# Gated mix of a state-space layer and a feed-forward layer: the first 512 rows of even x brought in by transposing DMAs

## The chip, the cores and the metric

The kernel runs on one core of a Trainium2 chip. The metric is device microseconds for one execution; the time before is the median of three runs. The profile is one execution of the same program, with times in microseconds from its span's start. PE is TensorE (PEld its weight loads), DVE is VectorE, ACT is ScalarE, POOL is GpSimd, SP is SyncE. SP and ACT each have a DMA queue; SPq and ACTq are the instructions that issue DMAs on them.

## The reference

x has 2048 rows of 448 columns, in bf16. Two branches read it and a gate mixes them:

```python
g = sigmoid((x * gate_w).sum(-1, keepdims=True))
# a: a complex diagonal state space; h runs over the 2048 rows
Lam_bar = exp(dt * Lam);  B_bar = ((Lam_bar - 1) / Lam)[:, None] * Bmat
h[t] = Lam_bar * h[t-1] + B_bar @ x[t]
a = 2 * real(C @ h) + x * Dskip
# b: feed-forward, F = 1792
b = silu(x @ w1) @ w2
return g * a + (1 - g) * b
```

## The kernel before

The rows of x are split into even and odd ones: `x2` has 1024 rows, each with an even row's 448 columns and then the odd row's. The tile XT holds x transposed (columns on the partitions): blocks 0 to 3 are the even columns 0 to 511, where block 3 holds 64 columns that count and 64 that belong to the odd half; blocks 4 to 7 are the odd ones. XR holds the 64 remaining columns on the other half of the partitions, so that two matmuls of 64 partitions can run side by side.

The instructions of each engine are written out by hand in program order. A small tracker (`Tracker`, L43) puts the waits: an operation waits for the last writer of each key that it reads, and for the readers of what it overwrites. DMAs are issued by SP or ACT, in the order in which the code names them, and each has a semaphore of its own.

PE's order is this. First come warm-up matmuls on constants (`warm`, L477). Then comes the first feed-forward matmul for the even rows 0 to 511 (chunk 0), for the first six blocks of 128 hidden columns, in six PSUM banks: `ffn1_first` (L427) runs the first three column blocks of x (j = 0, 1, 2), and `ffn1_rem` (L443) the remaining 64 columns, for two banks at a time, and starts the SiLU activation of them (L455, on ACT, into AT). After that the stream is made of pairs (`pair`, L373, with its matmuls at L365): the other hidden blocks of chunk 0, then chunk 1, then the state-space input projections of XT with BT (`bu_even`, `bu_odd`, `bu3_even`, `bu3_odd`) between them, and the second feed-forward matmul (L809, L794) and the output projection (L1047) behind. `mm_cols` (L469) puts three parameter rows (tile R: log_dt and the two halves of Lambda) on the partitions by four tiny matmuls inside `ffn1_first`. A chain of small DVE and ACT operations follows from them: PV (L528), dt, phf, ar, mag, and a table load for SiLU (L572).

In the head of the kernel before, natural x (rows on the partitions) for the first 512 even rows comes by six plain loads into XH, which is the first part of the tile XN, in pieces with the keys XA0 to XA3, XB0 and XB1, on the queues of SP and ACT in turn, with W1's first pieces between them (W1E, L259). PE turns each 128 x 128 tile of it (`turn_k`, L489, transposes at L491) into PSUM, and DVE copies the result into XT (`turned_k` L499, at L501; `turned_x` L504, at L507), and into XR (L571). Matmuls of `ffn1_first` stand between these transposes, the first of them on 256 columns of x only (h = 0, 1).

After the loads of the head, SP waits for the two W1 pieces of the remaining 64 columns (`gE`), and then issues all other transposing DMAs (`ldt`, L228, at L229): XT of even rows 512 to 1023 (XTe1, XTer1), the four of B into BT, XT of the odd rows (XTo0, XTr0, XTo1, XTr1). Between them stand the loads of natural x that are still missing (`load_xn`, L303): h = 0 brings the columns 512 to 895 of the first 512 rows of x2, after the BT transposes, and h = 1 the other 512 rows. Natural x is read by DVE for the gate (L650) and for the skip product (L658). The broadcast loads GWB and DB (`ld_b`, L297), which those two read, are issued on ACT's queue at the end of the head.

Of the kernel before, what the change touches and what calls it, by code (L numbers as in the profile page):

```python
# [8 lines left out]
AF = mybir.ActivationFunctionType  # L9

F32 = DT.float32
BF16 = DT.bfloat16
# [7 lines left out]
D = 448  # L20
# [2 lines left out]
NK = 1024  # L23
NKT = 8
NF1 = 6
NWARM = 20


class Dma:
# [121 lines left out]
def gated_mix(nc, A_x, A_Lambda_re, A_Lambda_im, A_B_re, A_B_im, A_C_re, A_C_im, A_log_dt,  # L151
              A_Dskip, B_x, B_w1, B_w2, gate_w, out):
    with ExitStack() as ctx:
        E = ctx.enter_context
        T = Tracker(nc, ctx)
# [76 lines left out]
        XE = [(["XTe000", "XTe001", "XTe010", "XTe011", "XTe02"], ["XTe03"]), (["XTe1"], ["XTer1"])]  # L232
        XO = [([f"XTo{h}"], [f"XTr{h}"]) for h in range(2)]

        def swap_xr(eng, h, odd):
# [18 lines left out]
        XA = ["XA0", "XA1", "XA2", "XA3", "XB0", "XB1"]  # L254
        FA, FB = 768, 1280
        x0 = x2[0:512, 0:512].rearrange("(k p) c -> p k c", p=128)
# [11 lines left out]
        def ld_wr(eng, c, later):  # L268
            p = slice(64 * c, 64 * c + 64)
            if later:  # L270
                return ld(eng, W1E[p, 3, 384:896].rearrange("p (n f) -> p n f", n=2),
                          B_w1[384:448, FA:].rearrange("p (n c f) -> p n c f", n=2, c=2)[:, :, c, :], f"W1Es{c}")
            return ld(eng, W1E[p, 3, 0:384], B_w1[384:448, 384 * c:384 * c + 384], f"W1Er{c}")

        for k, eng in enumerate(("sp", "act")):
            ld(eng, XH[:, k, 0:256], x0[:, k, 0:256], XA[k])
        for c, eng in enumerate(("sp", "act")):
            ld_w(eng, 0, 384 * c, 384 * c + 384, c)
        for k, eng in ((2, "sp"), (3, "act")):
            ld(eng, XH[:, k, 0:384], x0[:, k, 0:384], XA[k])  # L280
        ld_w("sp", 1)
        ld("act", XH[:, 0:2, 256:512], x0[:, 0:2, 256:512], XA[4])
        for i, (eng, v) in enumerate((("sp", A_log_dt), ("sp", A_Lambda_re), ("act", A_Lambda_im))):
            ld_row(eng, i, v)
        ld_w("act", 2)
        ld("sp", XH[:, 2:4, 384:512], x0[:, 2:4, 384:512], XA[5])
        gE = [ld_wr(eng, c, False) for c, eng in enumerate(("sp", "act"))]
        ld_w3("sp", 0, 2, FA, FB, "d")
        ld_w3("act", 2, 3, FA, FB, "d")
        for c, eng in enumerate(("sp", "act")):  # L290
            ld_wr(eng, c, True)
        T.op("act", lambda e: e.activation(JK[:, 0:1], HP[:, :], AF.Exp), reads=["HP"], writes=["JK0"])
        ld_w3("sp", 0, 1, FB, F_FF, "e")
        ld_w3("act", 1, 3, FB, F_FF, "e")
        BTK = [f"BT{i}" for i in range(4)] + ["BTz"]
# [1 line left out]
        def ld_b(dst, src, key):  # L297
            ld("act", dst[:, :], row(src).partition_broadcast(128).rearrange("p o n -> p (o n)"), key)

        ld_b(GWB, gate_w, "GW")  # L300
        ld_b(DB, A_Dskip, "DB")

        def load_xn(h):  # L303
            c0 = 0 if h else 512
            ld("sp", XN[:, 8 * h * D:8 * (h + 1) * D].rearrange("p (k c) -> p k c", k=4)[:, :, c0:],
               x2[h * 512:(h + 1) * 512, c0:].rearrange("(k p) c -> p k c", p=128), f"XN{h}")

        T.wait_all("sp", gE)
        ldt(XT[:, 0:3, 512:1024], x2[512:1024, 0:384], "XTe1")
# [116 lines left out]

        def ffn1_first():  # L427
            banks = [nxt() for _ in range(NF1)]
            for j, h in ((0, 0), (0, 1), (1, None), (2, None)):
                c = slice(0, 512) if h is None else slice(256 * h, 256 * h + 256)  # L430
                for n, fb in enumerate((0, 2, 4, 1, 3, 5)):
                    bank = banks[fb]
                    T.op("pe", lambda pe, fb=fb, bank=bank, j=j, h=h, c=c: pe.matmul(  # L433
                        ps[:, bank, c], W1E[:, j, ff(fb) * 128:(ff(fb) + 1) * 128], XT[:, j, c],
                        start=(h == 0), stop=(h == 0), skip_group_check=(h != 0)),
                        reads=[f"W1Ej{j}" if j else f"W1Ej0{fb % 2}"] + (
                            ["XTe02"] if j == 2 else [f"XTe0{j}{h}"] if h is not None else [f"XTe0{j}0", f"XTe0{j}1"]),
                        writes=[f"ps{bank}"])
                    if (j, h, n) in ((0, 0, 3), (0, 0, 5), (1, None, 2), (1, None, 5)):
                        yield  # L440
            yield banks

# [43 lines left out]
        PB = (6, 7, 6, 7)  # L486
        xp = [ps[:, b, 0:256].bitcast(BF16) for b in PB]

        def turn_k(j, k, b=None):  # L489
            b = PB[j] if b is None else b  # L490
            T.op("pe", lambda pe: pe.transpose(  # L491
                ps[:, b, 0:256].bitcast(BF16)[:, k * 128:(k + 1) * 128], XH[:, k, j * 128:(j + 1) * 128], ID[:, :]),
                reads=[XA[k if j < 2 or (j == 2 and k > 1) else 4 + k // 2], "ID"], writes=[f"ps{b}"])

        def turn_x(j, i):
            for k in (2 * i, 2 * i + 1):
                turn_k(j, k)

        def turned_k(j, k, b):  # L499
            c = slice(128 * k, 128 * k + 128)  # L500
            T.op("dve", lambda e: e.tensor_copy(XT[:, j, c], ps[:, b, 0:256].bitcast(BF16)[:, c]),  # L501
                 reads=[f"ps{b}"], writes=[f"XTe0{j}{k // 2}" + ("" if k % 2 else "a")])

        def turned_x(j, i=None, b=None):  # L504
            c, key = (slice(0, 512), f"XTe0{j}") if i is None else (slice(256 * i, 256 * i + 256), f"XTe0{j}{i}")
            b = PB[j] if b is None else b
            T.op("dve", lambda e: e.tensor_copy(XT[:, j, c], ps[:, b, 0:256].bitcast(BF16)[:, c]),  # L507
                 reads=[f"ps{b}"], writes=[key])

        for k in range(2):  # L510
            turn_k(0, k, 6 - k)
            turned_k(0, k, 6 - k)
        turn_x(1, 0)
        turned_x(1, 0)
        warm(2, 4)
        first = ffn1_first()
        next(first)
        for k in (2, 3):
            turn_k(0, k, k + 4)
            turned_k(0, k, k + 4)  # L520
        next(first)
        for k in (2, 3):
            turn_k(1, k, 6)
        turned_x(1, 1, 6)
        rd()
        next(first)
        T.op("pe", mm_cols, reads=["R0", "R1", "R2", "Rd", "ID"], writes=["pv"])
        T.op("dve", lambda e: e.tensor_copy(  # L528
            PV[:, :, :], ps[:, 7, 256:288].rearrange("p (t c) -> p t c", c=8)[:, :, 0:4]),
            reads=["pv", "ps7"], writes=["PV"])  # L530
        for i in range(2):
            turn_x(2, i)
        turned_x(2)
        next(first)
        for i in range(2):
            turn_x(3, i)

        names = {}

# [5 lines left out]
        def col(n):  # L545
            i = pc(n)
            return P[:, i, :]
# [7 lines left out]
        def pts(o, a, s1, s2, op0, op1, ra):  # L555
            T.op("dve", lambda e: e.tensor_scalar(col(o), a, s1, s2, op0, op1), reads=ra, writes=[o])
# [81 lines left out]
        def xblock(b):  # L638
            v = XN[:, 4 * b * D:4 * (b + 1) * D].rearrange("p (k c) -> p k c", k=4) if b > 1 else \
                XH[:, :, b * D:(b + 1) * D]  # L640
            return v, [*(XA if b < 2 else []), *([f"XN{b // 2}"] if b else [])]

        def block(tile):
            return tile // 4 if tile > 7 else tile % 2
# [516 lines left out]
        f = ffn1(2)  # L1161
# [100 lines left out]
```

## Time and profile before

| what | value |
|---|---|
| median of 3 runs | 136.64 us (136.61 to 136.76) |
| the profiled execution | 136.72 us |
| its span | 135.3 us |
| PE busy | 131.9 us, 97% |
| DVE busy | 114.2 us, 84% |
| ACT busy | 93.7 us, 69% |
| first warm-up matmul | 0.82 us |
| first matmul of ffn1_first | 3.80 us |
| first matmul of ffn1_rem | 9.79 us |

The chain that ended last is a list of pieces in order of time: what the last instruction waited for, followed back to the start. The windows give, for a stretch of time, the busy time of each engine with the number of its instructions, the granted share of the TensorE clock (PEclk), the mean busy share of the 16 DMA engines, which can exceed 1 where packets overlap, and what they moved in GB/s. The list of DMA issues gives the time from the issue to the landing.

### The profile page before, as it was taken

How to read it: one execution, taken by the hardware profiler on the slowest of the kernel's cores; microseconds unless marked ns; L12 is line 12 of the kernel's file. 1: busy time of each engine (PE TensorE's matmuls, PEld its weight loads, DVE VectorE, ACT ScalarE, POOL GpSimd, SP SyncE). 2: the span in 40 equal slices, each digit the busy share in tenths (PEclk: the TensorE clock that was granted, in tenths of full speed). 3: DMA queues.
4: the chain of work that ended last, by engine and by line, in shares of the span. 5: the costliest groups of instructions: out<-in, count | busy, mean ns of one | idle time of the engine just before them, and what ended most of it. 6: DMA issues, size and time to landing. Idle time of an engine off the chain costs nothing.

```text
span 135.3 us, 2630 instructions
## 1 busy us (share of the span) xinstructions
PE 131.9 (97%) x1072; PEld 65.7 (49%) x1073; DVE 114.2 (84%) x152; ACT 93.7 (69%) x146; POOL 15.1 (11%) x32
## 2 busy tenths in 40 slices
PE   7899999999999999999999999999999999999993
PEld 7554444444444554444445544445555555555552
DVE  1467898917899798999999999999999999994554
ACT  0369888899939999768999597797113437879200
POOL 7108768050000000000000000000000000000000
DMA  4999979999897220000122000000000000222123
GB/s 109 273 278 162 157 153 244 181 286 300 251 184 123 55 62 0 0 0 0 44 56 60 5 0 0 0 5 0 0 0 0 0 0 7 100 89 81 68 78 126
DMA packets 24928, 11.95 MB, mean 88 GB/s; under 512 B 16851, under 2 KB 24406, under 8 KB 24918
## 3 DMA queue, kind: packets, MB, share of 16 engines
q1 hardware_dynamic: 22996, 10.43, 32.3%
q10 hardware_dynamic: 1922, 1.37, 3.6%
q8 instruction: 8, 0.13, 0.4%
q14 instruction: 2, 0.02, 0.0%
HBM read 5.51 MB, written 1.84 MB: 54 GB/s over the span
## 4 chain that ended last, share of the span: by engine, by line
PE 94%; DMA 3%; DVE 1%; ACTq 1%; issue 0%
PE ps L365 44%; PE ps L794 16%; PE ps L809 16%; PE ps L1047 15%; DMA XN<-in_A_x_dram 3%; PE ps L433 3%; DVE TMPS L1071 1%; ACTq L226 1%; PE ps L491 1%; PE ps L447 1%; PE ps L472 0%
## 5 line engine op out<-in xcount | busy, mean ns | idle before, releaser
L365 PE MATMUL ps<-XT,W1E 64*128 64x512 bf16 x325 | 41.3, 376 | 0.0
L455 ACT ACTIVATE AT<-ps 128x1024 bf16<-128x1024 f32 x28 | 28.2, 1019 | 7.4 <-PE ps L365 7.2
L365 PEld LDWEIGHTS ps<-XT,W1E 64*128 64x128 bf16 x325 | 16.9, 94 | 19.0 <-ACT AT L455 0.3
L365 PE MATMUL ps<-XT,BT 64*128 64x512 bf16 x156 | 22.4, 376 | 0.0
L809 PE MATMUL ps<-W,AT 64*128 64x448 bf16 x224 | 21.5, 349 | 0.0
L794 PE MATMUL ps<-W,AT 128*128 128x448 bf16 x112 | 21.4, 353 | 0.0
L794 PEld LDWEIGHTS ps<-W,AT 128*128 128x128 bf16 x112 | 10.9, 98 | 10.5 <-issue 0.4
L809 PEld LDWEIGHTS ps<-W,AT 64*128 64x128 bf16 x224 | 10.9, 94 | 10.4
L838 ACT ACTIVATE BT<-ps,GT 128x448 bf16<-128x448 f32 x8 | 5.1, 634 | 13.2 <-PE ps L794 13.2
L894 DVE SCALAR_TENSOR_TENSOR HS<-VE,P,ps 128x512 bf16<-128x512 bf16 (+1 forms) x13 | 9.6, 780 | 3.9 <-PE ps L365 3.9
L365 PEld LDWEIGHTS ps<-XT,BT 64*128 64x128 bf16 x156 | 8.1, 94 | 9.3 <-DVE HS L894 0.4
L938 DVE TENSOR_TENSOR_SCAN G<-P,Q 128x1024 f32<-128x1024 f32 (+1 forms) x6 | 11.4, 1923 | 0.0
L1047 PE MATMUL ps<-CO,VE 128*128 128x448 bf16 (+2 forms) x63 | 11.1, 332 | 0.0
L1047 PE MATMUL ps<-CO,HS 128*128 128x448 bf16 x56 | 11.1, 352 | 0.0
L365 PE MATMUL ps<-XR,W1E 64*128 64x512 bf16 x25 | 9.2, 376 | 0.0
L1047 PEld LDWEIGHTS ps<-CO,VE 128*128 128x128 bf16 x63 | 6.0, 98 | 4.8
L1047 PEld LDWEIGHTS ps<-CO,HS 128*128 128x128 bf16 x56 | 5.5, 98 | 5.1
L891 DVE TENSOR_TENSOR Q<-G,COS 128x2048 bf16<-128x2048 f32 (+1 forms) x4 | 7.0, 1755 | 0.1
L891 DVE TENSOR_TENSOR Q<-G,SIN 128x2048 bf16<-128x2048 f32 (+1 forms) x4 | 7.0, 1750 | 0.0
L856 ACT ACTIVATE VE<-ps 128x1024 bf16<-128x1024 f32 x6 | 6.1, 1020 | 1.2 <-PE ps L365 1.2
L858 ACT ACTIVATE ps<-VE,P 128x1024 f32<-128x1024 bf16 x6 | 6.7, 1118 | 0.2
L894 DVE SCALAR_TENSOR_TENSOR VE<-HS,P,FP 128x512 bf16<-128x512 bf16 (+1 forms) x7 | 6.6, 976 | 0.1
(123 smaller groups left out, 179.1 us busy)
## 6 DMA issues: line engine op xcount, KB each, us to landing
W<-in_B_w_dram SPq DMA_DIRECT2D x2, 784.0 KB, 6.6
XN<-in_A_x_dram SPq DMA_DIRECT2D x1, 896.0 KB, 5.1
out_dram<-OT SPq DMA_DIRECT2D x8, 112.0 KB, 1.7
out_dram<-TMPS SPq DMA_DIRECT2D x7, 112.0 KB, 1.7
HS<-HS SPq DMA_DIRECT2D x4, 128.0 KB, 2.3
XN<-in_A_x_dram SPq DMA_DIRECT2D x1, 384.0 KB, 3.7
W1E<-in_B_w_dram SPq DMA_DIRECT2D x1, 256.0 KB, 5.5
W1E<-in_B_w_dram ACTq DMA_DIRECT2D x1, 256.0 KB, 5.0
```

The costliest lines, as they stand in the source:

```text
L365: ins = pe.matmul(ps[:, bank, :], w(p, j), xh(odd, h, j, p), start=start and j == js[0], stop=stop and j == js[-1], skip_group_check=seeded)
L433: T.op("pe", lambda pe, fb=fb, bank=bank, j=j, h=h, c=c: pe.matmul(ps[:, bank, c], W1E[:, j, ff(fb) * 128:(ff(fb) + 1) * 128], XT[:, j, c] ...
L455: T.op("act", lambda e: e.activation(a[:, fb:fb + n, :], ps[:, bank:bank + n, :], AF.Silu), reads=[f"ps{bank + i}" for i in range(n)], wri ...
L794: ins = pe.matmul(ps[:, bank, 0:D], a[:, fb, q * 128:(q + 1) * 128], W2[:, ff(fb), :], start=(first and fb == 0), stop=(fb == NFB - 1), sk ...
L809: ins = pe.matmul(ps[:, bank, 0:D], a[p, fb, q * 128:(q + 1) * 128], W2[p, ff(fb), :], start=(start and fb == 0), stop=(not start and fb = ...
L838: T.op("act", lambda e: e.activation(bs(tile), ps[:, bank, 0:D], AF.Copy, scale=sc), reads=[f"ps{bank}", "GT2" if h else "GRI"], writes=ks)
L856: T.op("act", lambda e: e.activation(VE[:, m:m + 2, hs], ps[:, b[0]:b[0] + 2, :], AF.Copy), reads=[f"ps{i}" for i in b], writes=vs)
L858: T.op("act", lambda e: e.activation(ps[:, o[0]:o[0] + 2, :], VE[:, m:m + 2, hs], AF.Copy, scale=c1("lr", pt)), reads=vs + ["lr"], writes= ...
L891: T.op("dve", lambda e: e.tensor_tensor(o, a, b, op), reads=reads, writes=writes)
L894: T.op("dve", lambda e: e.scalar_tensor_tensor(o, a, s, b, ALU.mult, ALU.add), reads=reads, writes=writes)
L938: T.op("dve", lambda e: e.tensor_tensor_scan(G[:, c, w], rb, Q1[:, c, w], init, ALU.mult, ALU.add), reads=[f"Q1{c}", "rr", f"G{c}"], write ...
L1047: ins = pe.matmul(ps[:, bank, c], state(kt, odd, m), CO[:, m, c], start=False, stop=(m == YB[-1]), skip_group_check=True)
```

## The change

Three transposing DMAs on SP's queue bring XT for the first 512 even rows: block 0 (key XTe00), block 1 (XTe01), and blocks 2 and 3 together (XTe02 and XTe03). The plain loads of natural x, the PE transposes and the DVE copies of the head go; one copy from XT to XR (`swap_xr` on DVE) comes in place of L571. W1's first pieces, the three R rows and the two 64-row pieces are all issued on ACT's queue, and the first table load (for Exp) moves ahead of the 64-row pieces. `ffn1_first` runs j = 0, 1, 2 on all 512 columns of x, with `mm_cols` after the third matmul of j = 1. The warm-up has 25 matmuls instead of 20. Natural x for the first 512 rows now comes whole, by two loads of 448 columns each (XN0, XN1), at the place where `load_xn(0)` stood. GWB and DB are issued on ACT behind the load of SiLU's table.

```diff
-NWARM = 20
+NWARM = 25
...
-        for k, eng in enumerate(("sp", "act")):
-            ld(eng, XH[:, k, 0:256], x0[:, k, 0:256], XA[k])
-        for c, eng in enumerate(("sp", "act")):
-            ld_w(eng, 0, 384 * c, 384 * c + 384, c)
-        for k, eng in ((2, "sp"), (3, "act")):
-            ld(eng, XH[:, k, 0:384], x0[:, k, 0:384], XA[k])
-        ld_w("sp", 1)
-        ld("act", XH[:, 0:2, 256:512], x0[:, 0:2, 256:512], XA[4])
-        for i, (eng, v) in enumerate((("sp", A_log_dt), ("sp", A_Lambda_re), ("act", A_Lambda_im))):
-            ld_row(eng, i, v)
-        ld_w("act", 2)
-        ld("sp", XH[:, 2:4, 384:512], x0[:, 2:4, 384:512], XA[5])
-        gE = [ld_wr(eng, c, False) for c, eng in enumerate(("sp", "act"))]
+        ldt(XT[:, 0:1, 0:512], x2[0:512, 0:128], "XTe00")
+        for c in range(2):
+            ld_w("act", 0, 384 * c, 384 * c + 384, c)
+        ldt(XT[:, 1:2, 0:512], x2[0:512, 128:256], "XTe01")
+        for j in (1, 2):
+            ld_w("act", j)
+        ldt(XT[:, 2:4, 0:512], x2[0:512, 256:512], "XTe02", also=["XTe03"])
+        for i, v in enumerate((A_log_dt, A_Lambda_re, A_Lambda_im)):
+            ld_row("act", i, v)
+        T.op("act", lambda e: e.activation(JK[:, 0:1], HP[:, :], AF.Exp), reads=["HP"], writes=["JK0"])
+        gE = [ld_wr("act", c, False) for c in range(2)]
         ld_w3("sp", 0, 2, FA, FB, "d")
         ld_w3("act", 2, 3, FA, FB, "d")
         for c, eng in enumerate(("sp", "act")):
             ld_wr(eng, c, True)
-        T.op("act", lambda e: e.activation(JK[:, 0:1], HP[:, :], AF.Exp), reads=["HP"], writes=["JK0"])
...
-        ld_b(GWB, gate_w, "GW")
-        ld_b(DB, A_Dskip, "DB")
-
         def load_xn(h):
-            c0 = 0 if h else 512
-            ld("sp", XN[:, 8 * h * D:8 * (h + 1) * D].rearrange("p (k c) -> p k c", k=4)[:, :, c0:],
-               x2[h * 512:(h + 1) * 512, c0:].rearrange("(k p) c -> p k c", p=128), f"XN{h}")
+            for c, key in (((slice(0, D), "XN0"), (slice(D, 2 * D), "XN1")) if h == 0 else ((slice(0, 2 * D), "XN2"),)):
+                ld("sp", XN[:, 8 * h * D:8 * (h + 1) * D].rearrange("p (k c) -> p k c", k=4)[:, :, c],
+                   x2[h * 512:(h + 1) * 512, c].rearrange("(k p) c -> p k c", p=128), key)
...
-            for j, h in ((0, 0), (0, 1), (1, None), (2, None)):
-                c = slice(0, 512) if h is None else slice(256 * h, 256 * h + 256)
+            for j in range(3):
                 for n, fb in enumerate((0, 2, 4, 1, 3, 5)):
...
-                    if (j, h, n) in ((0, 0, 3), (0, 0, 5), (1, None, 2), (1, None, 5)):
+                    if (j, n) == (1, 2):
                         yield
...
-        for k in range(2):
-            turn_k(0, k, 6 - k)
-            turned_k(0, k, 6 - k)
-        turn_x(1, 0)
-        turned_x(1, 0)
-        warm(2, 4)
         first = ffn1_first()
-        next(first)
-        for k in (2, 3):
-            turn_k(0, k, k + 4)
-            turned_k(0, k, k + 4)
-        next(first)
-        for k in (2, 3):
-            turn_k(1, k, 6)
-        turned_x(1, 1, 6)
         rd()
         next(first)
         T.op("pe", mm_cols, reads=["R0", "R1", "R2", "Rd", "ID"], writes=["pv"])
...
-        for i in range(2):
-            turn_x(2, i)
-        turned_x(2)
-        next(first)
-        for i in range(2):
-            turn_x(3, i)
...
         pact("mag", col("ar"), AF.Exp, ["ar"])
-        turned_x(3)
-        T.op("dve", lambda e: e.tensor_copy(XR[64:128, 0:512], xp[3][0:64, :]), reads=["ps7"], writes=["XR0a"])
+        swap_xr("dve", 0, 0)
         T.op("act", lambda e: e.activation(JK[:, 0:1], HP[:, :], AF.Silu), reads=["HP"], writes=["JK0"])
+        ld_b(GWB, gate_w, "GW")
+        ld_b(DB, A_Dskip, "DB")
```

More of the change, by code (lines that the diff above doesn't have):

```diff
@@ L230, in ldt @@
                          writes=[key, *also], group=group)
-        XE = [(["XTe000", "XTe001", "XTe010", "XTe011", "XTe02"], ["XTe03"]), (["XTe1"], ["XTer1"])]
+        XE = [(["XTe00", "XTe01", "XTe02"], ["XTe03"]), (["XTe1"], ["XTer1"])]
         XO = [([f"XTo{h}"], [f"XTr{h}"]) for h in range(2)]
@@ L253, in gated_mix @@
         XH = XN[:, 0:8 * D].rearrange("p (k c) -> p k c", k=4)
-        XA = ["XA0", "XA1", "XA2", "XA3", "XB0", "XB1"]
         FA, FB = 768, 1280
-        x0 = x2[0:512, 0:512].rearrange("(k p) c -> p k c", p=128)
         def ld_w(eng, j, f0=0, f1=FA, key=""):
@@ L428, in ffn1_first @@
             banks = [nxt() for _ in range(NF1)]
-            for j, h in ((0, 0), (0, 1), (1, None), (2, None)):
-                c = slice(0, 512) if h is None else slice(256 * h, 256 * h + 256)
+            for j in range(3):
                 for n, fb in enumerate((0, 2, 4, 1, 3, 5)):
                     bank = banks[fb]
[L433 to L438, printed above, removed]
-                    if (j, h, n) in ((0, 0, 3), (0, 0, 5), (1, None, 2), (1, None, 5)):
+                    T.op("pe", lambda pe, fb=fb, bank=bank, j=j: pe.matmul(
+                        ps[:, bank, :], W1E[:, j, ff(fb) * 128:(ff(fb) + 1) * 128], XT[:, j, 0:512],
+                        start=(j == 0), stop=(j == 0), skip_group_check=(j != 0)),
+                        reads=[f"W1Ej{j}" if j else f"W1Ej0{fb % 2}", f"XTe0{j}"], writes=[f"ps{bank}"])
+                    if (j, n) == (1, 2):
                         yield
@@ L485, in gated_mix @@
         warm(NWARM, 5)
[L486 to L508, printed above, removed]
-        for k in range(2):
-            turn_k(0, k, 6 - k)
-            turned_k(0, k, 6 - k)
-        turn_x(1, 0)
-        turned_x(1, 0)
-        warm(2, 4)
-        first = ffn1_first()
-        next(first)
-        for k in (2, 3):
-            turn_k(0, k, k + 4)
-            turned_k(0, k, k + 4)
-        next(first)
-        for k in (2, 3):
-            turn_k(1, k, 6)
-        turned_x(1, 1, 6)
+        first = ffn1_first()
         rd()
@@ L640, in xblock @@
                 XH[:, :, b * D:(b + 1) * D]
-            return v, [*(XA if b < 2 else []), *([f"XN{b // 2}"] if b else [])]
+            return v, [f"XN{min(b, 2)}"]
         def block(tile):
```

## The prediction

> **What bounds the kernel now.** I read the page's first part, then the chain of waits in order of time, then the timeline and the windows of the first 13 us.
>
> ```profile
> PE 131.9 (97%) x1072; PEld 65.7 (49%) x1073; DVE 114.2 (84%) x152; ACT 93.7 (69%) x146; POOL 15.1 (11%) x32
> ```
>
> PE is busy 97% of the span, so something can be won or lost only where PE is not yet fed. The chain says where that is:
>
> ```profile
> 1.71 3.59 DMA XN<-in_A_x_dram
> 5.30 0.05 issue
> 5.34 0.23 PE ps L491
> 5.57 0.22 PE ps L433 x2
> 5.79 0.11 PE ps L491 x2
> 5.90 1.47 PE ps L433 x9
> ...
> 8.56 1.29 PE ps L433 x6
> 9.86 0.76 PE ps L447 x6
> 10.61 31.76 PE ps L365 x294
> ...
> 112.05 20.71 PE ps L1047 x112
> ```
>
> Columns: start, duration, what. Until 5.30 the chain waits for a load of natural x. From there to the end it is matmuls without a hole: 294 row-paired matmuls in 31.76 are 147 x 0.216 us. So the whole question is when PE begins the first remainder matmul (ffn1_rem, L447, start 9.79 in the timeline). I call that moment P0; a shift of P0 shifts the end by as much, if no later wait opens.
>
> How fast the DMA engines feed this stretch, from the windows (last two columns: DMA share, GB/s):
>
> ```profile
> 2.00:4.00 2.00, 2.00 (x19) 1.57 (x17) 0.68 (x3) 0.00 (x0) 1.76 (x5) 1.00 1.00 254
> 8.00:10.00 2.00, 2.00 (x14) 0.89 (x14) 1.57 (x9) 1.64 (x3) 0.00 (x0) 1.00 1.00 279
> 10.00:12.50 2.50, 2.50 (x26) 1.09 (x24) 2.40 (x9) 2.33 (x6) 1.76 (x2) 1.00 0.74 109
> 22.00:24.00 2.00, 2.00 (x22) 0.88 (x18) 2.00 (x3) 1.61 (x3) 1.57 (x2) 1.00 1.21 277
> ```
>
> Plain loads alone run at 254 to 279, transposing loads nearly alone at 277. In 10.0 to 12.5, where SP's first transposes run beside the last plain loads of ACT's queue (GWB, DB), the two together reach 109. The changed head is such a mixture.
>
> **The change, part by part.** The profiled execution took 136.72 (span 135.3 and 1.42 around it), 0.08 over the median of 136.64. I work in the span's time and put the shift on the median.
>
> *TensorE.* Sixteen L491 transposes and two spare warm-up matmuls go. In the chain after 5.30 the transposes are 0.23+0.11+0.24+0.22 = 0.80 us. The 12 half-width and 12 full-width L433 matmuls become 18 full-width ones: the same columns. Six take 1.29 (row above), so a j step costs 1.30. Warm-up: 20 took 0.82 to 2.92 (next matmul), 0.105 each; 25 end at about 3.45. On PE alone this is a gain, but only if its input is there.
>
> *VectorE.* Nine copies (L501 4 x 0.225, L507 4 x 0.36, L571 0.42: 2.8 us) go; one XT to XR copy of 0.29 comes (row L238). It waits for the third transpose and stands before the phase columns; PE needs 1.30 for j=2 after the same landing, so 0.29 is hidden, and if that cover were gone it would cost 0.3.
>
> *The three transposes on SP* (T1, T2 of one 128-column block, T3 of two). The nearest rows when the queue is short: one block issues in 1.26 and lands 2.9 after its start (24.55), three blocks issue in 1.51 and land after 4.0 (23.00). T3 lies between: 1.38 and 3.45. Lower bound: T1 starts at 0.78 and lands 3.7; T2 starts 2.08, lands 5.0; T3 starts 3.38, lands 6.83.
>
> Upper bound by the shared engines. Before T3's last packet pass: x 512 KB, W1's head on ACT 576 KB, its 64-row pieces 96 KB, and, of the 128 KB piece issued beside T3, half: 1248 KB, 1.278 MB, from 2.0 us on (window 1.5:2.0 moves 24 GB/s, 2.0:2.5 246). At 279 GB/s this ends at 6.6, so the issue bound holds; at 109 it ends at 13.7. I take the middle, 194, since the 109 window holds pure mixing with a tail of two broadcast loads, and the head has wide W1 rows: 6.59 us, end 8.59. Landing follows the end of traffic by 0.4 (transposed traffic falls off in 26.75:27.00, landing 24.55+2.9 = 27.45). T3: 9.0. In the same way T1 (with the two 96 KB pieces) 2.0+1.69+0.4 = 4.1, T2 (with two 192 KB pieces) 6.8.
>
> Then PE: j=0 from 4.1, done by 5.8; j=1 6.85 to 8.15; j=2 from 9.05 to 10.35 = P0. Against 9.79: 0.56 later.
>
> *ACT's queue.* All W1 head loads and the three R rows now issue there, 0.45 and 0.3 each (rows 0.42, 0.45; 0.33, 0.22), the R rows from 2.65 to 3.5 instead of 2.64 to 3.26. They sit behind 576 KB, landing near 5 to 6.4 (before: the R copy L466 ran at 6.27); mm_cols needs them after the third matmul of j=1, 7.5. The chain from mm_cols (7.21) to the end of JK (10.05) is 2.84: PV, dt, mag, table load 1.28. So the first AT activation could run at 10.34; its matmuls end 10.35+0.43. Hidden; in the fast case below it is what binds. GWB and DB issue (0.49+0.45) moves behind the Silu load: 0.94 under a table load of 1.28, nothing; without the cover 0.9 on ACT. Their first reader is L650 at 23.51; landing took 5.4 and 5.9, from about 9.5 that is 15.4: hidden. The first table load (L292) moves ahead of the later W1 issues; ACT issued DMAs at 5.68 while that load ran from 5.61, so nothing waits.
>
> *SP's queue behind.* Issued behind T3 at 4.8: W1's 256 KB piece (before 4.34), needed 0.66 after P0 (10.45 - 9.79). Behind T3 at 194 to 279 GB/s it takes 0.94 to 1.35: lands about 10.3 against a need of 11.0. XTe1 waits for the 64-row pieces; issue from about 6.9 instead of 8.60, though its packets wait for the same bytes. It is needed at 15.85, landed 14.2: hidden. Natural x of block 0 is now 896 KB instead of 384: 524 kB more, 1.9 us at 277, on everything behind. XTr0 24.6 becomes 26.5, XTr1 27.45 becomes 29.3. Their XR copies are read by PE at 29.23 and 32.25 (timeline, the XR matmuls), and DVE stands idle 3.22 before 31.03. Cover 2.4 and 2.6 us: nothing; beyond it each us costs a us.
>
> Sum: +0.56, 136.64 + 0.56 = 137.2.
>
> **Two rules weighed.** The rows: 16 tiles (23.00 to 27.45) took 4.45 us, 0.28 a tile. The Trainium skill, "VectorE: DVE Perf Modes", The three transpose paths, gives 390 ns on TensorE and 1309 ns by DMA for a 128x128 tile, which speaks against the change; sixteen in a row would be an estimate of 20.9 us and P0 some 14 us later. The row is five times faster, so I do not use it. The other way: alone, transposes ran at 277 GB/s, mixed at 109. The Trainium skill, "Advanced Engine Details and Errata", X-Bar Transpose (TRN2), says that transposes are as fast as regular DMAs, 350 to 400 GB/s expected; by it my sum would be the issue bound, a gain. Here the transposes keep pace with plain loads when alone (277 beside 279, short of that figure), and neither does in the mixture.
>
> **Rivals.** *Transposes flow as alone (faster).* T3 at 6.83, j=2 ends 8.18. Then ACT binds: j=0 from 3.75 with two matmuls at the early half speed (0.43) ends 5.5, mm_cols 6.15, activation from 9.0, its banks free at 10.0; PE asked for them 1.52 after P0 (11.31): P0 counts as 8.5. Gain 1.3: 135.35. For: 277 alone, and the ACT queue leaves gaps. Against: the 109 row. It decides if T3 lands before 8.4.
>
> *W1's 256 KB piece keeps its 5.5 us (same).* Issue 4.8 + 5.5 (DMA issues) = 10.3 against 10.45 now: whatever T3 does up to 8.3, the next pair starts 0.15 earlier: 136.5.
>
> *Cold clock (slower).* Before, matmuls came every 0.105 until about 4.2 and twice as fast after (256 columns in 0.109 in the timeline's 5.89 row); the granted clock reads 1.00 throughout. PE now idles between 3.45 and T1. If the fast pace is delayed past j=1, j=0 is 4.1 to 6.7, j=1 to 9.4, j=2 to 10.7: +0.9, 137.55. It decides if T1 lands past about 4.2.
>
> **How the numbers follow.** Shared engines 0.50 and cold clock 0.07 make slower 0.57; flowing as alone 0.33 makes faster; the W1 piece 0.10 makes same. The bound of 0.2% is 0.27 us, about what a measurement of this kernel can tell from no change. The range runs from the fast case, 135.4, to the mixture at 156 GB/s (T3 at 10.6, P0 11.95, +2.16), 138.8; the rate of 109 throughout (142 and more) is left out. The slower cases' own range is 136.9 to 138.8.
>
> **What would show it.** After: three DMA_TRANSPOSE on SP from 0.78 to about 4.8; the T3 wait ahead of j=2 in the chain as "DMA XT" ; windows 2:9 below 250 GB/s; the first L436 matmul at 10.35; from there PE without a hole. Wrong if that matmul comes before 9.5, if PE waits for W1E instead of XT, or if new waits on XR or XN show past 20 us.

## The result, and the profile after

The changed kernel takes 138.06 us (median of 4 runs, 137.86 to 138.85) beside 136.62 us (136.41 to 136.76) for the kernel before: ratio 1.0116, 95% interval 1.0093 to 1.0138. It is slower, by 1.3 to 1.9 us. Ratios, here and below, leave out runs in a slow state, which lie well above the others of the same kernel, so a ratio can differ from that of the medians. The profiled execution took 137.86 with a span of 136.6 (before: 136.72 and 135.3).

The first part of the page of the changed kernel shows that TensorE does as much work as before in a longer span; VectorE has less:

```profile
PE 131.7 (96%) x1054; PEld 64.4 (47%) x1054; DVE 112.1 (82%) x144; ACT 93.7 (69%) x146; POOL 13.3 (10%) x32
```

The chain of waits of the changed kernel (start, duration, what); landings of single DMAs, here and below, are those that the trace gives for each issue:

```profile
2.06 5.70 DMA XT<-in_A_x_dram
7.75 0.14 issue
7.89 0.81 PE ps L424 x3
8.70 0.13 issue
8.82 0.24 PE ps L461 x4
9.06 1.96 PE ps L424 x9
11.03 0.75 PE ps L436 x6
11.78 31.88 PE ps L357 x294
```

The chain waits for T2, the second transposing DMA (5.70 from its issue to 7.75), not for T3, whose landing the trace puts at 8.53. Behind T2 come j=1, the parameter columns (L461) and j=2, and then the same 294 paired matmuls as before (31.88 beside 31.76). One short hole is left, and it holds a second wait: the small 0.13 ahead of L461. The timeline shows it (TensorE's matmuls and VectorE's copy of the parameter rows; a bracket gives the idle time ahead and its releaser):

```profile
4.33 2.35 PE L424 MATMUL ps<-XT,W1E 128*128 128x512 bf16 x6 [0.69 <-DMA XT<-in_A_x_dram]
7.89 0.81 PE L424 MATMUL ps<-XT,W1E 128*128 128x512 bf16 x3 [1.20 <-DMA XT<-in_A_x_dram]
8.40 0.17 DVE L455 COPY R<-R 3x64 bf16<-3x64 bf16 x1 [6.96 <-DMA R<-in_A_Lambda_re_dram]
8.82 0.24 PE L461 MATMUL ps<-ID,R 128*128 128x4 bf16 x4
...
8.92 2.10 PE L424 MATMUL ps<-XT,W1E 128*128 128x512 bf16 x9
...
10.96 0.39 PE L436 MATMUL ps<-XT,W1E 64*128 64x512 bf16 x1
```

In the trace the three matmuls from 7.89 start 0.215 apart, so L461 could have started at 8.54. It started at 8.82, behind the copy of the rows, which landed at 7.94 and 8.31. The wait that ended last in the head is thus the one for the rows, 0.28 behind the one for T2.

The first remainder matmul, P0, comes at 10.96 instead of 9.79: 1.17 later. The next difference is the wait of weight loads for the first SiLU activation (0.43 instead of 0.32 on the two timelines): 0.11. Together 1.28, and the spans differ by 1.3. Nothing later adds to it.

The windows (columns: window, length, busy time and count of PE, PEld, DVE, ACT and POOL, granted clock, DMA share, GB/s). First the kernel before, for stretches not shown so far:

```profile
4.00:6.00 2.00, 1.49 (x11) 0.84 (x10) 0.51 (x3) 0.39 (x1) 0.13 (x2) 1.00 0.94 293
6.00:8.00 2.00, 1.95 (x19) 1.34 (x20) 0.85 (x4) 1.31 (x3) 0.00 (x0) 1.00 0.94 275
```

And the changed kernel:

```profile
2.00:4.00 2.00, 1.64 (x16) 1.38 (x13) 0.00 (x0) 0.00 (x0) 1.76 (x5) 1.00 0.96 255
4.00:6.00 2.00, 1.67 (x5) 0.58 (x6) 0.00 (x0) 1.49 (x2) 0.13 (x2) 1.00 1.17 146
6.00:8.00 2.00, 0.80 (x4) 0.27 (x3) 0.00 (x0) 0.00 (x0) 0.00 (x0) 1.00 1.20 202
8.00:10.00 2.00, 1.87 (x12) 0.71 (x11) 0.68 (x5) 0.31 (x2) 0.00 (x0) 1.00 1.12 302
2.00:7.00 5.00, 4.00 (x22) 2.10 (x19) 0.00 (x0) 1.49 (x2) 1.89 (x6) 1.00 1.13 192
```

While transposing and plain loads are in flight together the engines are fuller (share 1.17) and move half as much (146 beside 293). The rate recovers as the last transposes end: 245 from 7 to 8 us, 305 from 8 to 9.

### The profile page after: what moved, and what is told of

Same layout as the page of the kernel before. It is cut to its first block, busy times and chain, and to the rows that moved or that the text cites. A ratio compares the mean times of both kernels' runs of the same rounds, so it can differ in the third digit from the quotient of the medians.

```text
span 136.6 us, 2579 instructions
## 1 busy us (share of the span) xinstructions
PE 131.7 (96%) x1054; PEld 64.4 (47%) x1054; DVE 112.1 (82%) x144; ACT 93.7 (69%) x146; POOL 13.3 (10%) x32
## 4 chain that ended last, share of the span: by engine, by line
PE 92%; DMA 4%; SPq 1%; DVE 1%; issue 0%
PE ps L357 43%; PE ps L740 16%; PE ps L755 16%; PE ps L993 15%; DMA XT<-in_A_x_dram 4%; PE ps L424 2%; SPq L229 1%; DVE TMPS L1017 1%; PE ps L436 1%; PE ps L461 0%
## 5 line engine op out<-in xcount | busy, mean ns | idle before, releaser
L740 PEld LDWEIGHTS ps<-W,AT 128*128 128x128 bf16 x112 | 10.9, 98 | 10.5 <-issue 0.4
L755 PEld LDWEIGHTS ps<-W,AT 64*128 64x128 bf16 x224 | 10.9, 94 | 10.4
L784 ACT ACTIVATE BT<-ps,GT 128x448 bf16<-128x448 f32 x8 | 5.1, 634 | 13.2 <-PE ps L740 13.2
L993 PE MATMUL ps<-CO,VE 128*128 128x448 bf16 (+2 forms) x63 | 11.1, 332 | 0.0
L993 PE MATMUL ps<-CO,HS 128*128 128x448 bf16 x56 | 11.1, 352 | 0.0
L424 PE MATMUL ps<-XT,W1E 128*128 128x512 bf16 x18 | 5.3, 438 | 1.9 <-DMA XT<-in_A_x_dram 1.9
```

Source lines behind the costliest of these rows:

```text
L424: T.op("pe", lambda pe, fb=fb, bank=bank, j=j: pe.matmul(ps[:, bank, :], W1E[:, j, ff(fb) * 128:(ff(fb) + 1) * 128], XT[:, j, 0:512], star ...
L740: ins = pe.matmul(ps[:, bank, 0:D], a[:, fb, q * 128:(q + 1) * 128], W2[:, ff(fb), :], start=(first and fb == 0), stop=(fb == NFB - 1), sk ...
L755: ins = pe.matmul(ps[:, bank, 0:D], a[p, fb, q * 128:(q + 1) * 128], W2[p, ff(fb), :], start=(start and fb == 0), stop=(not start and fb = ...
L784: T.op("act", lambda e: e.activation(bs(tile), ps[:, bank, 0:D], AF.Copy, scale=sc), reads=[f"ps{bank}", "GT2" if h else "GRI"], writes=ks)
L993: ins = pe.matmul(ps[:, bank, c], state(kt, odd, m), CO[:, m, c], start=False, stop=(m == YB[-1]), skip_group_check=True)
```

## The experiments

**Theories.** M: the three transposes and W1's plain loads, in flight together, share the engines at a low rate; the transposes land late, and P0 with them. Q: it is the new assignment of the loads to the two queues, and transposing costs nothing by itself. Others are named where they are tested. The kernel before, in the runs beside the experiments, took 136.44 to 136.60.

**1. The transposes without W1 beside them** (one run).

```diff
-        for j in (1, 2):
-            ld_w("act", j)
-        ldt(XT[:, 2:4, 0:512], x2[0:512, 256:512], "XTe02", also=["XTe03"])
+        gT = ldt(XT[:, 2:4, 0:512], x2[0:512, 256:512], "XTe02", also=["XTe03"])
         ...                                  # the three rows
+        T.wait_all("act", [gT])
+        for j in (1, 2):
+            ld_w("act", j)
```

> The changed kernel, but ACT waits for the landing of the third transpose before it issues the W1 pieces of j = 1 and j = 2, so the transposes run beside the two 96 KB pieces of j = 0 only. Theory M (transposes and plain loads that share the 16 DMA engines slow each other): the second transpose lands within 3.4 us of its issue (by 5.5, not 7.75) and the third by 7.2 (not 8.53). Rival Q (transposes are slow by themselves at the start of a program, or one queue issues them too slowly): the second still lands after 7. In both the kernel itself is later, since W1 comes after 9: first remainder matmul at 11.5 to 12.5, 138.4 to 139.6 us.

T1 landed at 4.49, T2 at 5.03 and T3 at 6.75 (changed kernel: 4.20, 7.75 and 8.53). The prediction's issue bound was 3.7, 5.0 and 6.83. So the second and third transposes by themselves are not slow; M holds on this point. In time the kernel came to 142.43, more than expected. Its chain:

```profile
6.78 3.22 DMA W1E<-in_B_w_dram
9.99 0.05 issue
10.04 1.46 PE ps L425 x3
11.50 0.09 PE ps L462 x4
11.59 3.86 PE ps L425 x9
```

Twelve matmuls take 1.46 + 3.86 = 5.3 us where they take 2.6 at 0.216 each: TensorE ran at half speed in all three steps: in j=0 (six matmuls in 2.72 from 4.63 on), and again behind an idle stretch of 2.69 us. The full pace came only at about 15.8. That was not in the expectation; whether the idle stretch did it is not shown, since the pace was already half before it.

**2. The queues without the transposes**: the kernel before, with all loads of x on SP and W1's head and the rows on ACT (6 runs).

```diff
-        for k, eng in enumerate(("sp", "act")):
-            ld(eng, XH[:, k, 0:256], x0[:, k, 0:256], XA[k])
-        for c, eng in enumerate(("sp", "act")):
-            ld_w(eng, 0, 384 * c, 384 * c + 384, c)
+        for k in range(2):
+            ld("sp", XH[:, k, 0:256], x0[:, k, 0:256], XA[k])
+        for c in range(2):
+            ld_w("act", 0, 384 * c, 384 * c + 384, c)
...                                           # XA2, XA3, XB0, XB1 on SP; W1 j=1, 2, rows, 64-row pieces on ACT
```

> The kernel before with the queues of the changed one and nothing else of it: all six natural x loads on SP, the first W1 pieces, the R rows and the two 64-row pieces on ACT; x still turned by TensorE. Theory M: plain loads on both queues mix well, the first remainder matmul stays between 9.4 and 10.4 (before 9.79), 136.3 to 137.2 us. Rival Q (W1 on one queue is what makes the head late): remainder matmul at 10.8 or later, 137.6 us or more.

139.22 (137.63 to 139.86), ratio 1.0147 (1.0095 to 1.0199). M's number was missed and Q's was met, but not for Q's reason alone. Windows of this run:

```profile
4.00:6.00 2.00, 0.94 (x7) 0.41 (x5) 0.30 (x2) 0.00 (x0) 0.13 (x2) 1.00 0.93 298
...
8.00:10.00 2.00, 1.88 (x12) 1.00 (x12) 0.26 (x2) 0.21 (x1) 0.00 (x0) 0.50 1.03 261
```

The engines kept their rate (298). What changed is the order of bytes: W1's 192 KB pieces, now near the head of a queue without x, were served together with x, and XA3 landed at 6.37 instead of 5.30. TensorE stood idle 0.97 and 0.50 us for XA2 and XA3, and then the granted clock fell to 0.50 (8 to 10 us, seventh column of numbers: PEclk). Two causes in one run; experiment 3 takes them apart.

**3. The same, with TensorE kept busy** (6 runs).

```diff
         for k in (2, 3):
+            warm(9 if k == 2 else 4, 5)
             turn_k(0, k, k + 4)
```

> The queue experiment (plain loads, all of x on SP, W1's head on ScalarE's queue) with 9 and 4 extra warm-up matmuls in the two stretches in which TensorE was idle there (0.97 and 0.50 us before 5.69 and 6.41). If the lower granted clock at 7 to 11 us that stood behind that kernel's 139.2 came from those idle stretches, the spacing of the matmuls stays at about 0.11 and 0.22, XA3 still lands at about 6.4 (1.1 later than before), P0 comes at 10.8 to 11.2, the time is 137.4 to 137.9, and the two clusters of times (137.7 and 139.5) become one. If the clock drops for another reason (the load on TensorE itself), spacing 0.43 stays and the time stays at 139 or rises.

137.72 (137.16 to 137.82), ratio 1.0084 (1.0066 to 1.0102). The clock stayed at 1.00 from 2 to 12 us, and the times no longer fall into two groups (in experiment 2: 137.63 and 137.86, and four from 139.18 to 139.86). So the idle stretches stood behind the fall of the clock and the slower group. In the profiled run, the fastest of the six (137.16), XA3 landed at 5.89 and P0 was 10.38: 0.59 later than before in both, though earlier than expected (6.4; 10.8 to 11.2). The time is as expected. That run moved 293 GB/s from 2 to 7 us:

```profile
2.00:7.00 5.00, 4.67 (x45) 3.57 (x43) 1.54 (x7) 0.48 (x1) 1.89 (x6) 1.00 0.98 293
```

By the ratios (1.0084 beside 1.0116) a loss of about three quarters of that of the change therefore arises with plain loads at the full rate, from the queue assignment (and 13 spare matmuls). The trace accounts for 0.59 of it, in the fastest run. M is not the only way to lose.

This run also shows what the mixture does, since its queues carry the same loads of W1 at the same places as those of the changed kernel, and only x comes without a transpose. The packet records of the traces give the time of each packet. The 1536-byte packets of W1's two 192 KB pieces took 67 ns on average here and 142 in the changed kernel. The 256-byte packets of the three transposes took 27 ns there and 18.5 in experiment 1, with little beside them. The median packet is the same each time (65 and 18 ns): most packets go at full pace, and in some stretches, as from 4.8 to 5.2 us of the changed kernel, both kinds stand almost still together. So the transposes and the plain loads delay each other.

**4. No idle TensorE in the head**: the changed kernel with `NWARM = 34` (6 runs).

> The changed kernel with 34 warm-up matmuls, so that TensorE has no idle time before the first transpose lands (they end near 4.5, it landed at 4.20). Theory M: the second transpose decides, j = 0 may run at 0.216 us a matmul in place of 0.427 but j = 1 starts at 7.9 as before: 138.0 us, within 0.3. Rival C (the cold clock after the idle time is what costs): j = 0 ends near 5.9, and the end moves by 0.5 to 0.8: 137.3 to 137.5 us.

137.76 (137.46 to 138.24), ratio 1.0092 (1.0071 to 1.0112); P0 10.89. TensorE:

```profile
4.45 2.41 PE L424 MATMUL ps<-XT,W1E 128*128 128x512 bf16 x6
7.64 0.81 PE L424 MATMUL ps<-XT,W1E 128*128 128x512 bf16 x3 [0.78 <-DMA XT<-in_A_x_dram]
8.75 0.24 PE L461 MATMUL ps<-ID,R 128*128 128x4 bf16 x4 [0.30 <-DVE R L455]
```

j=0 starts without any idle time and still takes 2.41 for six matmuls (half speed); j=1 waits for T2 (7.50) all the same. The slow j=0 is real and hidden. The 0.30 is the wait for the row loads, which landed at 7.83 and 8.24: L461 could have followed at 8.29 and came at 8.75. T2 came 0.25 earlier than in the changed kernel, and the rows took most of that back.

**5. The rows first**: the changed kernel with ACT's row loads ahead of W1's j=1 and j=2 (5 runs).

```diff
+        for i, v in enumerate((A_log_dt, A_Lambda_re, A_Lambda_im)):
+            ld_row("act", i, v)
         for j in (1, 2):
             ld_w("act", j)
         ldt(XT[:, 2:4, 0:512], x2[0:512, 256:512], "XTe02", also=["XTe03"])
-        for i, v in enumerate((A_log_dt, A_Lambda_re, A_Lambda_im)):
-            ld_row("act", i, v)
```

> The changed kernel with ScalarE's three row loads (log_dt, Lambda) issued before W1's j=1 and j=2 pieces instead of behind them. Theory M (the second transposing DMA, landed 7.75, sets the end; the rows cost only the 0.13 us that VectorE's copy of them kept TensorE waiting in the changed kernel's trace): the rows land at 5 to 6.5, the two W1 pieces about 0.3 us later and still before TensorE needs them, the 0.13 goes and nothing else: 137.8 to 138.0, first matmul of the remaining tiles (P0) at 10.8 to 11.0. Rival R (the late rows are the term that decides, since they landed at 7.94 and 8.31 where 5 to 6.4 was predicted): P0 falls by more than 0.5, time 137.5 or less.

137.72 (137.56 to 138.06), ratio 1.0095 (1.0078 to 1.0111); P0 10.90. Time and P0 are about where M put them (137.8 to 138.0; 10.8 to 11.0), and the inside is not:

```profile
0.78 4.08 DMA XT<-in_A_x_dram
4.86 0.14 issue
4.99 3.80 PE ps L424 x9
8.79 0.08 PE ps L461 x4
8.87 2.10 PE ps L424 x9
```

The rows landed at 5.05 and 5.25. Their three issues hold up W1's j=1 and j=2 pieces, issued at 2.83 and 3.28 instead of 1.68 and 2.16. T2 landed at 5.97, 1.8 earlier than in the changed kernel, but T1 came at 4.86 (4.20) and T3 at 9.38 (8.53). TensorE, idle for 1.35 us before T1, then ran nine matmuls in 3.80, and j=2 started at 9.52, 0.14 after T3's landing. Now T3 is the wait that ends last, with the nine slow matmuls close behind it (they would have let j=2 start at 9.38), and P0 stays at 10.9. So no single transfer "is" the loss: with one wait gone, the next stands at almost the same place. The rate was again low (207 GB/s from 2 to 7, 192 in the changed kernel). That T3 was late because T2 was early is a reading of this one trace, not shown.

**6. Shorter rows in W1's loads**: the changed kernel, with the j=1 and j=2 pieces cut in two (768 bytes a row; the matmuls wait for both halves) (6 runs).

```diff
-            ld_w("act", j)
+            ld_w("act", j, 0, 384, "x")
+            ld_w("act", j, 384, 768, "")
```

> The changed kernel with the W1 pieces of j = 1 and j = 2 each cut into two loads of 384 columns (rows of 768 bytes, not 1536), same queue, same bytes. Theory M1 (what slows the transposes is sharing the engines with a plain load at all): 4 to 7 us still near 150 GB/s, second transpose after 7, 137.7 to 138.5 us. Theory M2 (long rows on the other queue hold each engine while the transposes wait for it): more than 200 GB/s there, second transpose by 6.5, 137.3 us or less.

138.85 (138.43 to 139.97), ratio 1.0167 (1.0132 to 1.0202). Neither expectation was met whole: the rate stayed low (197 and 159 in 4:6 and 6:8), as M1 says, but T2 landed before 7 (6.62) and the time is above M1's. T3 (9.14) and the rows (9.11, 9.81) landed later. Row length does not cure the mixture; it shifts who waits. In the traced run, the slowest of the six (139.97), most of the further loss is in the head: TensorE waited 1.50 us for the copy of the rows, whose issues stood behind four pieces instead of two, and P0 was 12.46. XTe1 was issued at 11.19 (changed kernel 9.80), and this delay ran through SP's queue to a transfer 18 us later:

```profile
29.33 4.75 DMA XT<-in_A_x_dram
...
34.42 1.42 DVE HS L841 x2
```

There TensorE waited 0.36 us for HS. Here the cover of the last transposing load is used up, which the prediction named and which the changed kernel did not reach.

**7. The order of need on one queue**: the changed kernel with 34 warm-ups and all of W1 behind j=0 on SP, j=1 between T2 and T3, j=2 behind T3, the rows right behind j=0 on ACT (6 runs).

```diff
+        ld_w("sp", 1)
         ldt(XT[:, 2:4, 0:512], x2[0:512, 256:512], "XTe02", also=["XTe03"])
...
+        ld_w("sp", 2)
+        gE = [ld_wr("sp", c, False) for c in range(2)]
```

> The changed kernel with all W1 loads but the two pieces of j = 0 on SP's queue, in the order in which TensorE needs them (transpose, transpose, W1 j = 1, double transpose, W1 j = 2, then the rest), so that transposes and plain loads follow each other and do not share the engines; 34 warm-up matmuls. Theory M: second transpose by 5.5, third by 7.8, W1 j = 2 by 8.5; first remainder matmul at 9.3 to 10.2 (in the changed kernel 10.96); 136.3 to 137.3 us. Rival (SP's issue of 1.3 us per transpose, or the start of the program, is the limit): third transpose after 8.5, remainder matmul after 10.8, 137.8 us or more.

142.75 (140.66 to 143.69), ratio 1.037 (1.0316 to 1.0425). In the traced run, the slowest of the six (143.69), the head did what M says: T2 5.41, T3 7.76, P0 10.17. Then:

```profile
9.02 6.09 DMA W1E<-in_B_w_dram
...
15.25 33.94 PE ps L357 x288
```

The later W1 pieces, alone on SP and beside ACT's two broadcasts (landed 13.2 and 14.9), came only by 14.1 to 16.3, and TensorE stopped for 3.61 us.

**8. The same, broadcasts later**: GWB and DB issued behind the third AT activation (6 runs).

```diff
         ffn1_rem(first, 4)
+        ld_b(GWB, gate_w, "GW")
+        ld_b(DB, A_Dskip, "DB")
```

> The one-queue experiment (142.75) with ScalarE's two broadcasts, GWB and DB, issued behind the first three AT activations (about 11.5 us) instead of at 8.5 and 8.9. If the broadcasts were what held back the last W1 pieces (landed 14.1 to 16.3) there, those land by 12.5, TensorE does not stop after P0 = 10.2, and the time is 136.9 to 137.4: the order of bytes in the head repairs about two thirds of the change's loss, and what is left is P0 10.2 against 9.79. If one queue by itself is too slow for the late W1 pieces, they land after 13 again and the time is 140 or more.

141.19 (139.95 to 142.57), ratio 1.0309 (1.0276 to 1.0342). Half of the expectation held: with the broadcasts issued at 10.61 and 11.00, the W1 pieces landed at 11.1 to 13.25, the stop of 3.61 us is gone, and P0 is 9.74, as early as in the kernel before. The last of these pieces came later than expected (12.5), and the time is in the rival's range, but not for the rival's reason: the next transfer was late:

```profile
10.85 7.67 DMA XT<-in_A_x_dram
...
18.57 28.23 PE ps L357 x244
```

XTe1 stands behind all W1 issues on SP (10.85; before 8.60), then runs beside the broadcasts and needs 7.67 us (before: issued at 8.60, landed at 14.15, 5.55). Windows of that stretch:

```profile
14.00:16.00 2.00, 2.00 (x22) 1.08 (x20) 1.00 (x3) 1.24 (x2) 0.77 (x1) 1.00 1.14 89
16.00:18.00 2.00, 0.54 (x6) 0.04 (x2) 0.00 (x0) 1.02 (x1) 0.00 (x0) 1.00 1.49 195
18.00:20.00 2.00, 1.43 (x8) 0.58 (x10) 0.00 (x0) 0.00 (x0) 0.00 (x0) 0.66 1.26 68
```

Again a share above 1 with 89 and 68 GB/s, with 195 between. Only the first two stretches are a mixture: the last broadcast landed at 18.57. And again the granted clock falls after TensorE's idle time (2.03 us).

**9. More natural x**: the kernel before with 448 KB more loaded into an unused part of W2's tile at the place of `load_xn(0)` (12 runs).

```diff
+            if h == 0:
+                T.dma("sp", lambda e: e.dma_start(W2[:, 0:4, :], x2[0:512, 0:D].rearrange("(k p) c -> p k c", p=128)),
+                      writes=["W20"])
```

> The kernel before with 448 KB more on SP's queue at the place where the changed kernel loads natural x: a load of the first 512 rows of even x into space that W2 fills later (nobody reads it, and it holds up nothing but the queue). Theory that the larger natural x is hidden by the idle time of VectorE: 136.6 us, within 0.25; the XR copies (L238) 1.3 to 1.9 us later, VectorE's wait before the first HS operation shorter by as much, TensorE without a hole. Rival N (the delay passes through to the end): 137.2 us or more.

136.61, ratio 1.0001 (0.9981 to 1.002). The last transposing load landed at 29.97 instead of 27.5. VectorE waited for XT (2.9 us in all instead of 0.2) in place of an idle time of its own, ahead of HS (1.4 instead of 3.9), and TensorE did not wait: hidden, as predicted.

**10 and 11. Smaller first loads in the kernel before.** XA2 and XA3 cut from 384 to 256 columns; the rest in XB1, ahead of the row loads (first version, 12 runs) or in XB1's old place (second, 11 runs); the transposes wait for the keys accordingly.

```diff
-            ld(eng, XH[:, k, 0:384], x0[:, k, 0:384], XA[k])
+            ld(eng, XH[:, k, 0:256], x0[:, k, 0:256], XA[k])
...
-        ld("sp", XH[:, 2:4, 384:512], x0[:, 2:4, 384:512], XA[5])
+        ld("sp", XH[:, 2:4, 256:512], x0[:, 2:4, 256:512], XA[5])
```

> The kernel before with its third and fourth x loads cut from 384 to 256 columns and the last x load widened to 256 and moved ahead of the R rows: 64 KB fewer before the load that ends the first chain (XA3, landed 5.30). If the order of bytes alone sets the head: XA3 lands 0.1 to 0.3 earlier, and the end by 0.1 to 0.2: 136.4 to 136.5 us. If TensorE's own work from 5.9 on is what counts, or the last x piece comes later: 136.6 us or more.

> The kernel before with the loads XA2 and XA3 cut from 384 to 256 columns, and the columns they lose carried by XB1, which stays in its place behind the row loads. Theory M (in plain loads the order of bytes sets the head, and nothing else): XA3 at 4.2 to 4.4 instead of 5.30, the row loads at 6.0 to 6.3 as before instead of 7.27, columns transposed at 7.2 or a little earlier, XB1 as late as 7.4 to 7.6 and so the start of j=2 about where it was; P0 9.6 to 9.9, time 136.4 to 136.8. Rival: the rows bound the head already before, so that an earlier XA3 is worth nothing and the larger XB1 costs 0.1 to 0.3.

First: 137.06, ratio 1.0026 (1.0008 to 1.0045). XA3 landed at 4.25 instead of 5.30, but the rows behind at 7.27 (6.25), and these took over: the chain has `DMA R` until 7.27, P0 is 10.19. Second: 136.61, ratio 1.0014 (1.0002 to 1.0026): XA3 4.61, rows 5.99, P0 9.29. The profiled run, the fastest of its eleven, took 136.22, as 0.50 less in P0 asks; the median does not show the gain, and the other runs left no trace. No version here beats the kernel before.

**A miss.** An earlier form of experiment 9, the kernel before with the head's natural x loaded a second time into its own place, took 156.94, because TensorE's transposes waited 19.1 us for that second load. It says nothing on any theory.

```diff
+            if h == 0:
+                T.dma("sp", lambda e: e.dma_start(XH[:, :, 0:512], x0[:, :, :]), writes=XA)
```

> The kernel before with 512 KB more on SP's queue where the changed kernel loads natural x: the 512 columns that it already has are loaded a second time (the result is the same). Theory that the later and larger natural x is hidden: 136.6 us, within 0.25, with the copies L238 of XR and what follows up to 1.9 us later on VectorE but no hole on TensorE. Rival N (it passes through): 137.2 us or more.

## Why the prediction was right, and where its sizes were off

**Where the time is lost: right.** P0 shifts and the rest follows. P0 +1.17 and one activation wait +0.11 make the span's +1.3. The size was off: +0.56 was forecast and +1.44 measured (by the medians), two and a half times as much.

**The rate: close, with luck.** The sum used 194 GB/s, the middle between 279 and 109. The changed kernel moved 192 from 2 to 7 us and 204 from 2.0 to 8.1; the kernel before 269 from 2 to 7. The end of traffic was put at 8.59 and T3 at 9.0; T3 landed at 8.53, and in experiments 4 to 6 at 8.49, 9.38 and 9.14. That mixing lowers the rate is shown by experiment 3 (293 with the same queues and plain loads) and by the packets. But the row of 109 is not "pure mixing": the first transposed packet of that stretch starts at 10.72, and the DMA share from 10.0 to 11.5 is 0.53, so for much of it there was little to move. That the middle between it and 279 came out within 1% is luck. Experiment 1 answers the first rival: transposes that flow as alone would have given its 6.83.

**The path in the head: not the one of the sum.** The sum let T3, at 9.0, release j=2. T3 came earlier than that and nobody waited for it: from 8.53, by the steps of the trace, P0 would have been about 10.06 (an estimate: 0.14 to the first matmul, 1.08 to the last start, 0.31 to P0). What held j=2 back was j=1, by two terms that were mis-sized.

- *T2.* "T2 (with two 192 KB pieces) 6.8" was 7.75. The sum counted only what was issued ahead of T2 and beside it on ACT. But T2 and T3 landed 0.78 apart: T3's traffic was served along with T2's. By 7.75 some 1.14 MB had moved (an estimate: 5 us at 192 GB/s and 0.75 at 245), not the 0.85 MB of that sum. A share of the engines is not a place in a line. j=1 began at 7.89 instead of 6.85.
- *The rows.* Placed at 5 to 6.4, they landed at 7.94 and 8.31. They too were counted by the bytes ahead of them only. VectorE's copy ended at 8.57, and the parameter columns began at 8.82 instead of 8.54: 0.28. The four matmuls of the columns took 0.10 more, which the sum had at nothing.

So j=2 began at 9.57 instead of 9.05: 0.52 of the miss of 0.61 in P0 (10.96 against 10.35). The other 0.09 is the step from full to row-paired matmuls: in the kernel before the last L433 starts at 9.48 and L447 at 9.79, 0.31 where full ones start 0.216 apart. It stands in both kernels; the prediction's own timeline had it.

**The activation chain: called hidden, and just not.** From mm_cols to the end of JK it took 2.81 (8.82 to 11.63), as the prediction read it (2.84). But mm_cols came at 8.82 instead of 7.5, so the first AT activation followed JK at 11.53, where its matmuls would have allowed about 11.39. That is the 0.11. In experiment 5, where mm_cols came at 8.63, the wait of the weight loads is 0.32 again.

Experiment 5 took the wait for the rows away and gained next to nothing, since T3 then ended last. T2 and the rows are the terms of this trace; the loss does not hang on them alone.

**Cold clock.** T1 landed at 4.20, at the edge of its condition (past about 4.2), and j=0 took 2.35 where six such matmuls at full pace take 1.46 on the timeline. It cost nothing, since T2 came later still. In experiment 4 warm-ups up to T1's landing did not change it; in experiments 7 and 8, with the same 34, the full pace was there by 5.1. In experiment 5, where T1 came at 4.86, it filled the stretch that T2 had freed.

**The W1 piece as the limit.** The 256 KB piece on SP needed 4.7 us instead of 5.5 and landed at 9.45, before P0. That rival did not occur.

**What was called hidden.** Natural x: experiment 9. The last transposing load came at 31.65 instead of 29.3. VectorE's waits for XT ahead of the XR copies grew from 0.2 to 2.1 us, still without a hole on TensorE, inside the 2.6 us that the prediction still counted and the 1.3 by which its readers moved; experiment 6 shows where it ends. GWB and DB landed at 14.0 and 15.9 and were first read at 25.80 and 26.99.

**What stays open.** The prediction named the mixture as the price. Experiment 3 shows that the queue assignment by itself, with plain loads at 293 GB/s, already costs 0.7 to 1.0%, which the prediction had not considered. In the changed kernel both act, on the same landings: at 293 GB/s its 1.278 MB would end at 2.0 + 4.4 = 6.4, an estimate by which the low rate is needed for its late T3; but experiment 8 reaches P0 9.74 with transposes issued in the order of need. How the 1.17 divides between rate and order is not settled: no run had the transposes in the changed order at the full rate. Nor does a low rate need the mixture: in the kernel before, with no plain load in flight (the last broadcast landed at 12.65, the next plain load was issued at 19.01), transposes moved 130 GB/s from 14 to 15 us and 43 from 15 to 16. Why is not shown.

## What to carry to other kernels

Where a head is fed by DMA, count what is in flight together, not only what is ahead in the queue: here T2, T3, the second W1 piece and even the three rows of 0.9 KB all landed between 7.4 and 8.6. Queues that carry one kind of load each lose the order that the interleaved lists had, and in this head transposing DMAs beside plain loads lowered the rate of both. Before moving work from TensorE to the DMA engines, look at the DMA share of that stretch: here it was already 0.94, and the 0.80 us of TensorE's transposes was the cheaper side.

## What the runs showed of the hardware

- Transposing and plain loads together: 141, 151 and 158 GB/s from 4 to 7 us of the changed kernel at a share of 0.96 to 1.38, where plain loads alone made 251 to 323 in the kernel before. The packets of both kinds took longer on average (142 ns instead of 67, 27 instead of 18.5). A high DMA share is no sign of a high rate. The Trainium skill, "Advanced Engine Details and Errata", X-Bar Transpose (TRN2), says that transposes are as fast as regular DMAs; experiment 1 does not speak against that for transposes with little beside them (T3 landed at 6.75, at the bound by its issue); in the mixed stretch, at 192 GB/s beside 293, neither is as fast as plain loads alone.
- Two forms of a slow TensorE. At the start matmuls of 512 columns come every 0.427 while the granted clock reads 1.00, even with TensorE busy from 0.82 to about 6 us (experiment 4); in experiment 1 so up to about 15.8, with idle stretches of 0.98 and 2.69 us. The number of warm-ups does not settle when this ends: with 34 of them the pace doubled at about 3.7 us in experiment 7 and at about 6.2 in experiment 4. The Trainium skill, "TensorE: Matmul & The Clock Gate", Part 1, gives 426.7 ns for 512 columns in the cold state and 215.7 in the warm one; both appear here (0.427, 0.216). The other form shows in the column: 0.50 for several us after idle stretches in experiments 2, 7 and 8, although 1.20 us of idle time in the changed kernel left it at 1.00. Thirteen spare matmuls kept it at 1.00 in experiment 3.
- A load earlier in one place came back later in another in experiments 5, 6, 8 and 10: with the engines nearly full from 2 to 10 us, the landings of the head trade places. Experiment 11 is an exception in its one trace: XA3, the rows and XB1 (6.86 instead of 7.27) all landed earlier.
